# Turning q and k of head groups 7 to 23 on TensorE with the identity instead of by DMA transposes

## The chip, the cores and the metric

The kernel runs on one core of a Trainium2 chip. The metric is the device time of one execution in microseconds. The engines are named as in the profile: PE (TensorE, matrix products, with PEld for its weight loads), DVE (VectorE), ACT (ScalarE), POOL (GpSimd) and SP (SyncE, which only issues DMAs here).

## The reference

An attention with normalised q and k, followed by a two-layer network with a leaky activation:

```python
batch, n_heads, seq, head_dim = (8, 12, 448, 64)
def rmsnorm(x, g):
    rms = np.sqrt(np.mean(x * x, axis=-1, keepdims=True) + 1e-06)
    return x / rms * g
q_n, k_n = (rmsnorm(q, g_q), rmsnorm(k, g_k))
scores = scale * np.matmul(q_n, k_n.transpose(0, 1, 3, 2))     # scale = 1/8
attn = np.exp(scores - scores.max(-1)); attn = attn / (attn.sum(-1) + 1e-09)
x = np.matmul(attn, v)             # (8, 12, 448, 64) -> (3584, 768)
h = x @ w_in                       # w_in (768, 2048)
g = np.maximum(h, 0.0) + alpha * np.minimum(h, 0.0)
out = g @ w_out                    # w_out (2048, 768), out float32 (3584, 768)
```

## The kernel before

The 12 heads of each of the 8 batch entries are taken two pairs at a time as *head groups* of four heads; three groups make one batch entry, so there are 24 groups, numbered 0 to 23 (`NG`; `G` is 3). In a tile of q or k the 128 partitions are two heads by 64, and the 448 positions of the sequence are these 64 by `J` = 7.

For each group, q and k are loaded to `nat` by SP, squared by POOL (`square`), summed by DVE (`reduce`, line 185), turned into reciprocal roots by ACT (`root`), and multiplied with them by POOL into fp16 tiles `qs` (`scale`, line 205). The scores need them with the head dimension on the partitions, so q and k are *turned* into `qT` and `kT`; kT also takes the gain g_q * g_k. Then `score` makes the scores of one key block in PSUM (`sc`, line 357), `soft` takes their exp on ACT (`expT`, line 371), the denominators are sums by TensorE with a column of ones (`dn`, `dnb`), their reciprocals come from a log and an exp on ACT (`rden`), and `attv` makes the attention's product (`av`, `avb`) that DVE multiplies into `xT` (lines 464, 481).

The network is worked in between. An *up product* (`up`) is six matmuls for 128 of the 2048 inner columns and one batch entry (`hT`, line 496), then on ACT a product with alpha into gT (line 536) and on DVE a maximum with hT into gT (line 540). An *output product* is 16 matmuls (`op`, line 558) or, for most tiles, eight at a time in a scheme that saves one product in eight with sums made beforehand (`quad_a`, `quad_b`, `quad_c`: `qx`, `qz`, `qc`, line 623), copied or added out of PSUM by DVE (`osb`) and stored by SP.

The order is written out by hand, for every engine the order in the program is the order in which it works. The main loop runs over *steps* `n`. A step has two to four score blocks (`bursts`), perhaps a denominator (`dens`) and an attention product (`avs`), and then a list of network products (`gaps`), which a planner shares out by cost. `turn_at` gives the step in which a group is turned: as a rule the last step before the one with its first scores; `turns` is the same by step. `jobs` hangs small work of other engines behind network products; `late` holds back a score's exp or a group's roots until so many up products are issued.

PSUM has three pools: `pss` with two buffers of two banks for the scores, `psf` with two single banks tagged `mm`, and `psa` with one buffer of two banks tagged `acc`. Products take an `mm` bank; where the step's plan calls them `spare` they take an `acc` bank instead, and their names get an "a" (`hTa`, `opa`, `qxa`, `qza`, `qca`). Denominators (`dn`) and attention products (`av`) take `acc` too.

Groups 0 to 6 are turned by TensorE: seven transposes of 128 by 128 for q and seven for k against an identity, into PSUM, from where DVE copies q (line 337) and k with the gain (line 339). From group `TD` = 7 on (17 groups) `turn_dma` issues two transposing DMAs on SP right after the multiplications in program order (line 304), and `turn` only multiplies kT in place with the gain on DVE (line 315). In the steps of the first seven turns the planner lends no spare bank; in those of the others it does.

Of the kernel before, what the change touches and what calls it, by code (L numbers as in the profile page):

```python
# [9 lines left out]
FP32 = mybir.dt.float32  # L10
FP16 = mybir.dt.float16
AF = mybir.ActivationFunctionType
ALU = mybir.AluOpType
# [8 lines left out]
def kernel(  # L22
# [12 lines left out]
    nc = tc.nc  # L35

    B, H, S, D = q.shape
    DM = H * D
    DF = moe_w_in.shape[1]
    J = S // 64  # L40
    HH = H // 2
    G = HH // 2
# [3 lines left out]
    W = 2 * S  # L46
    NG = B * G
    FB = DF // 4
    TD = min(7, NG)
    EB = 3  # L50
    EARLY = 3 * G
    PRE = 3 * G - 1
# [145 lines left out]
    def scale(y, nm):  # L198
        if y in (1, 3, 5):
            t = lent(HB + 4 * NB4 + "qk".index(nm) * NB4 // 2, NB4 // 2).bitcast(FP16)  # L200
            t = t.rearrange("p (j h d) -> p j h d", j=J, h=2)
        else:
            t = ld.tile([128, J, 2, D], FP16, name="qs", tag="qs", bufs=2)
        eng = nc.vector if y < G or (y, nm) == (G, "q") else nc.gpsimd
        eng.tensor_mul(  # L205
            out=t.rearrange("p j h d -> p h j d"),
            in0=nat[y, nm],
            in1=rr_t[y][:, "qk".index(nm)].unsqueeze(3).broadcast_to((128, 2, J, D)),
        )
        qs[y, nm] = t  # L210
# [30 lines left out]

    def part_scale(nm, j, n, eng):
        if (0, nm) not in qs:
            qs[0, nm] = ld.tile([128, J, 2, D], FP16, name="qs", tag="qs", bufs=2)
        eng.tensor_mul(
            out=qs[0, nm][:, j].rearrange("p j h d -> p h j d"),
            in0=nat[0, nm][:, :, j],
            in1=rr_t[0][:, "qk".index(nm), :, j].unsqueeze(3).broadcast_to((128, 2, n, D)),
        )
# [9 lines left out]

    def part_copy(nm, j, eng):  # L260
        if (0, nm) not in qkT:
            qkT[0, nm] = att.tile([128, J, 2, 64], FP16, name=f"{nm}T", tag=f"{nm}T", bufs=3)
        o = qkT[0, nm].rearrange("p j g c -> p j (g c)")[:, j]
        tp = tops["ps", nm][:, j]
        if nm == "k":
            nc.vector.tensor_scalar(
                out=o, in0=tp, scalar1=gain[:, 0:1], scalar2=None, op0=ALU.mult
            )
        elif eng is nc.scalar:
            nc.scalar.copy(out=o, in_=tp)  # L270
        else:
            eng.tensor_copy(out=o, in_=tp)

    mark = cst.tile([128, 1], FP16, name="mark", tag="mark")
    mark32 = cst.tile([128, 1], FP32, name="mark32", tag="mark32")

    def follow(y, nm):

# [2 lines left out]
    def turn_one(y, nm):  # L281
        t = psf.tile([128, 512], FP32, name="tps", tag="mm")
        tp = t[:, :S].bitcast(FP16).rearrange("p (j c) -> p j c", j=J)
        for j in range(J):
            nc.tensor.transpose(
                tp[:, j, :], qs[y, nm][:, j].rearrange("p h d -> p (h d)"), ident
            )
        t = att.tile([128, J, 2, 64], FP16, name=f"{nm}T", tag=f"{nm}T", bufs=3)
        o = t.rearrange("p j g c -> p j (g c)")
        if nm == "q":  # L290
            nc.vector.tensor_copy(out=o, in_=tp)
        else:

            for c in (slice(0, 2), slice(2, J)):
                nc.vector.tensor_scalar(
                    out=o[:, c], in0=tp[:, c], scalar1=gain[:, 0:1], scalar2=None,
                    op0=ALU.mult,
                )
        qkT[y, nm] = t

    def turn_dma(y):
        for nm in "qk":
            t = att.tile([128, J, 2, 64], FP16, name=f"{nm}T", tag=f"{nm}T", bufs=3)
            nc.sync.dma_start(
                out=t.rearrange("p j g c -> p j (g c)"),
                in_=qs[y, nm].rearrange("p j h d -> p (j h d)"),
                transpose=True,
            )
            qkT[y, nm] = t

    def turn(y):

        if y >= TD:
            t = qkT[y, "k"].rearrange("p j g c -> p (j g c)")
            nc.vector.tensor_scalar(  # L315
                out=t, in0=t, scalar1=gain[:, 0:1], scalar2=None, op0=ALU.mult,
                op1=ALU.max, accum_out=mark32,
            )
            return
        if y <= G:  # L320
            ps = [psf.tile([128, 512], FP32, name="tps", tag="mm") for _ in "qk"]
        else:
            ps2 = psa.tile([128, 2, 512], FP32, name="tps2", tag="acc")
            ps = [ps2[:, 0], ps2[:, 1]]
        tps = [
            t[:, : S].bitcast(FP16).rearrange("p (j c) -> p j c", j=J) for t in ps
        ]
        for tp, nm in zip(tps, "qk"):
            for j in range(J):
                nc.tensor.transpose(  # L330
                    tp[:, j, :], qs[y, nm][:, j].rearrange("p h d -> p (h d)"), ident
                )
        for tp, nm in zip(tps, "qk"):
            t = att.tile([128, J, 2, 64], FP16, name=f"{nm}T", tag=f"{nm}T", bufs=3)
            o = t.rearrange("p j g c -> p j (g c)")
            if nm == "q":
                nc.vector.tensor_copy(out=o, in_=tp)
            else:
                nc.vector.tensor_scalar(
                    out=o, in0=tp, scalar1=gain[:, 0:1], scalar2=None, op0=ALU.mult  # L340
                )
            qkT[y, nm] = t
# [4 lines left out]
    def pre(ys):  # L347
        return len(ys) == 1 and ys[0] >= PRE and ys[0] % G == G - 1
# [428 lines left out]
    while m < NG * J or steps:  # L777
        n = len(bursts)
# [38 lines left out]
    def after(n, f, *a):  # L817
        post.setdefault(max(int(n), 0), []).append((f, a))

    turn_at = {  # L820
        y: max(n for n in range(first_in[y]) if y >= TD or n not in dens)
        for y in range(1, NG)
    }
    turn_at[2], turn_at[G] = 5, av_at[0]
    turn_at.update(
        (y, den_at[y - 2] - pre((y - 2,))) for y in range(TD, NG) if y % G == 1
    )
    turns = {n: y for y, n in turn_at.items()}
    jobs, root_at, nexts = {}, {}, {}
    for y in range(G, NG):  # L830
# [54 lines left out]
    def cost(n):  # L885
        return (
            0.31 + 0.19 * len(bursts[n])
            + (0 if n not in dens else 0.4 if pre(dens[n]) else 1.35)
            + 1.35 * len(avs.get(n, ())) + (0.9 if turns.get(n, TD) < TD else 0.0)
        )  # L890

    def wide(n):
# [152 lines left out]
    for n in range(NB):  # L1045
# [70 lines left out]
        if n in roots:  # L1116
            y = roots[n]
            work = [(root, (y,)), (scale, (y, "q")), (scale, (y, "k"))]
            if lead:

                late = [(2, score, tiles[2]), (2, soft, tiles[2])]
            if y == 2 * G:
                late += [(3, f, a) for f, a in work]
            elif lead or wait and y < TD:
                late += [(2 if lead else 1, f, a) for f, a in work]
            else:
                for f, a in work:
                    f(*a)
            if y >= TD:
                turn_dma(y)  # L1130
        if n in nexts:
            load_qk(nexts[n])
        if n in dens and not lead and not sums:
# [5 lines left out]
        done = 0  # L1139

        spare_at, clock = [], 0.0
        taken = n + 1 in dens or n + 1 in avs or turns.get(n + 1, TD) < TD
        for k, (f, a) in enumerate(gaps[n]):
            free = 2.9 if sums else 2.3 if n in dens else (0.1, 1.2, 0.0)[len(avs.get(n, ()))]
            since += 1
            if clock >= free and not turns.get(n, TD) < TD and (
                since > 2 and not (taken and k == len(gaps[n]) - 1) or free == 0.0 and k == 0
            ):
                spare_at.append(k)
                since = 0  # L1150
            clock += UP if f is up else DOWN
        ups_first = gaps[n] and gaps[n][0][0] is up
        if ups_first and n in dens and not lead:
            for f, a in jobs.pop(n, ()):
                f(*a)
        turned = n in turns and gaps[n] and (turns[n] >= TD or turns[n] <= 2 * G)
        if turned and not ups_first and turns[n] >= TD:
            jobs.setdefault(n, []).append((turn, (turns[n],)))
        elif turned:
            turn(turns[n])  # L1160
        for k, (f, a) in enumerate(gaps[n]):
            spare = k in spare_at or f is up and a in forced
            if f is down:
                down(*a, jobs.pop(n, ()), spare)
            elif f is not up:
                f(*a, jobs.pop(n, []))
            else:
                f(*a, spare)
                done += 1
                if n in jobs and not (lead and done < 5) and (  # L1170
                    n < av_at[2 * G - 1] or done % 2
                ):
                    g, c = jobs[n].pop(0)
                    g(*c)
                    if not jobs[n]:
                        del jobs[n]
                while late and done == late[0][0]:
                    _, g, c = late.pop(0)
                    g(*c)
# [50 lines left out]
```

## Time and profile before

| | |
|---|---|
| median of 3 runs | 413.47 us (413.19 to 415.29) |
| profiled execution | 414.78 us |
| its span, first to last instruction | 413.0 us |
| mean granted TensorE clock | 0.995 |
| transposing DMAs | 17 of q, 17 of k; 2.9 and 3.7 us from issue to landing (median) |

Lines of the page that help to read it further, the costliest groups of instructions (line, engine, operation, out<-in, count, then busy us and mean ns of one, then idle time before them and what ended it):

```profile
L371 ACT ACTIVATE expT<-sc 128x896 f16<-128x896 f32 x168 | 147.8, 913 | 55.4 <-PE sc L357 55.0
L496 PE MATMUL hT<-xT,w_in_sb 128*128 128x448 f16 x546 | 113.7, 353 | 0.4 <-DVE gT L540 0.2
L205 POOL TENSOR_TENSOR qs<-nat,rr 128x896 f16<-128x896 f32 x36 | 60.9, 1713 | 33.4 <-issue 24.9
```

The busy time of one engine is no time on the path by itself: what matters is which engine the others wait for. ACT waits 55 us in total for scores.

### The profile page before, as it was taken

What the parts mean: (1) busy time and instruction counts of PE and PEld (TensorE: products, weight loads), DVE (VectorE), ACT (ScalarE), POOL (GpSimd) and SP (SyncE); (2) the same over time, 40 slices, a digit from 0 to 9 for tenths busy, and PEclk for the clock granted to TensorE, in tenths of its full rate; (3) what the DMA queues carried; (4) which work ended last, traced back from release to release, by engine and by line L of the source; (5) the groups of instructions that cost most, each with busy time, mean ns of one, the idle gap of its engine ahead of it and who ended that gap; (6) DMA issues with size and microseconds to landing.
All of it is one profiled execution on the core that took longest, in us unless ns stands there. A gap on an engine that the chain in (4) does not pass through costs nothing.

```text
span 413.0 us, 11724 instructions
## 1 busy us (share of the span) xinstructions
PE 398.9 (97%) x5055; PEld 208.1 (50%) x5055; DVE 266.9 (65%) x420; ACT 257.3 (62%) x390; POOL 255.8 (62%) x184
## 2 busy tenths in 40 slices
PE   7889999899999999999999999999999999999996
PEld 3344445444456445554455445545555455645664
DVE  3876875476567388785688585958576755465322
ACT  5697787567846785557766786875657783135110
POOL 5599996589677969376373847484724407300870
PEclk9899999999999999999999999999999999999999
DMA  8999899957754894329861697279332700320143
GB/s 259 231 217 206 172 200 155 248 169 103 163 81 134 204 169 91 115 63 197 144 168 48 173 138 177 63 180 193 59 75 54 127 3 24 75 59 0 30 103 97
DMA packets 67330, 53.38 MB, mean 129 GB/s; under 512 B 34880, under 2 KB 66768, under 8 KB 67280
## 3 DMA queue, kind: packets, MB, share of 16 engines
q1 hardware_dynamic: 53344, 40.45, 40.5%
q0 software_dynamic: 13536, 11.81, 21.5%
q8 instruction: 39, 0.64, 0.7%
q10 hardware_dynamic: 400, 0.39, 0.3%
q14 instruction: 11, 0.09, 0.1%
HBM read 45.62 MB, written 11.01 MB: 137 GB/s over the span
## 4 chain that ended last, share of the span: by engine, by line
PE 49%; DVE 6%; ACT 0%; issue 0%; DVEq 0%
PE hT L496 14%; PE hTa L496 7%; PE qx L623 5%; PE sc L357 3%; PE oq L623 3%; PE qc L623 3%; PE qz L623 2%; PE av L382 2%; PE oqm L623 2%; PE avb L382 1%; PE dn L382 1%; PE oqa L623 1%; DVE ss L185 1%; DVE xT L481 1%; DVE kT L315 1%; PE qza L623 1%
## 5 line engine op out<-in xcount | busy, mean ns | idle before, releaser
L371 ACT ACTIVATE expT<-sc 128x896 f16<-128x896 f32 x168 | 147.8, 913 | 55.4 <-PE sc L357 55.0
L496 PE MATMUL hT<-xT,w_in_sb 128*128 128x448 f16 x546 | 113.7, 353 | 0.4 <-DVE gT L540 0.2
L496 PEld LDWEIGHTS <-w_in_sb 128*128 128x128 f16 x768 | 72.7, 98 | 74.8 <-issue 10.1
L540 DVE TENSOR_TENSOR gT<-hT,gT 128x448 f16<-128x448 f32 x91 | 56.6, 623 | 40.1 <-ACT gT L536 39.2
L205 POOL TENSOR_TENSOR qs<-nat,rr 128x896 f16<-128x896 f32 x36 | 60.9, 1713 | 33.4 <-issue 24.9
L536 ACT ACTIVATE gT<-hT,cols 128x448 f16<-128x448 f32 x90 | 56.9, 633 | 33.9 <-PE hT L496 33.7
L177 POOL TENSOR_TENSOR sq<-nat 128x896 f32<-128x896 f32 x32 | 53.1, 1681 | 38.0 <-DMA nat<-in_q_dram 25.3
L357 PE MATMUL sc<-qT,kT 64*32 64x448 f16 (+1 forms) x1092 | 53.3, 358 | 3.5 <-ACT expT L371 1.1
L623 PEld LDWEIGHTS <-gT 128*128 128x128 f16 x352 | 33.4, 98 | 26.0 <-issue 4.9
L496 PE MATMUL hTa<-xT,w_in_sb 128*128 128x448 f16 x210 | 45.4, 352 | 0.0
L185 DVE TENSOR_REDUCE ss<-sq 128x14 f32<-128x896 f32 (+1 forms) x37 | 38.3, 1052 | 0.6 <-POOL sq L177 0.6
L481 DVE TENSOR_TENSOR xT<-av,rden 64x448 f16<-64x448 f32 (+1 forms) x37 | 27.2, 734 | 13.5 <-PE av L382 5.5
L536 ACT ACTIVATE gT<-hTa,cols 128x448 f16<-128x448 f32 x35 | 22.2, 635 | 19.1 <-PE hTa L496 19.1
L540 DVE TENSOR_TENSOR gT<-hTa,gT 128x448 f16<-128x448 f32 x35 | 21.8, 624 | 17.7 <-ACT gT L536 17.6
L357 PEld LDWEIGHTS <-kT 64*32 64x32 f16 (+1 forms) x1092 | 15.6, 93 | 34.7 <-issue 29.3
L558 PE MATMUL op<-w_out_sb,gT 128*128 128x384 f16 x160 | 27.4, 326 | 0.0
L382 PEld LDWEIGHTS <-vt 64*32 64x32 f16 x1344 | 20.2, 92 | 14.1 <-issue 5.0
L611 POOL TENSOR_TENSOR gs<-gT 128x1024 f16<-128x1024 f16 x3 | 6.4, 2121 | 30.3 <-DVE gT L540 28.1
L558 PEld LDWEIGHTS <-gT 128*128 128x128 f16 x192 | 18.0, 98 | 13.5 <-issue 2.4
L382 PE MATMUL av<-expT,vt 64*32 64x448 f16 x896 | 24.3, 350 | 0.3 <-DVE osb L671 0.3
L619 POOL TENSOR_TENSOR gT<-gT 128x1024 f16<-128x1024 f16 x11 | 23.8, 2166 | 0.0
L623 PE MATMUL qx<-w_out_sb,gT 128*128 128x384 f16 x120 | 20.9, 326 | 0.0
(148 smaller groups left out, 494.1 us busy)
## 6 DMA issues: line engine op xcount, KB each, us to landing
out_dram<-osb SPq DMA_DIRECT2D x107, 96.0 KB, 2.8
nat<-in_k_dram SPq DMA_DIRECT2D x21, 448.0 KB, 5.4
nat<-in_q_dram SPq DMA_DIRECT2D x20, 448.0 KB, 4.9
vt<-in_v_dram POOLq DMA_DIRECT2D x8, 672.0 KB, 11.0
w_in_sb<-in_moe_w_in_dram POOLq DMA_DIRECT2D x24, 128.0 KB, 5.0
w_out_sb<-in_moe_w_out_dram POOLq DMA_DIRECT2D x4, 768.0 KB, 10.8
arena<-in_q_dram SPq DMA_DIRECT2D x3, 448.0 KB, 7.8
arena<-in_k_dram SPq DMA_DIRECT2D x3, 448.0 KB, 8.5
```

Of the source, the lines that this page charges most:

```text
L177: nc.gpsimd.tensor_mul(out=sqf[:, c], in0=src[:, c], in1=src[:, c])
L185: nc.vector.tensor_reduce(out=o[:, c], in_=sqs[y, nm][:, c], axis=AXIS_X, op=ALU.add)
L205: eng.tensor_mul(out=t.rearrange("p j h d -> p h j d"), in0=nat[y, nm], in1=rr_t[y][:, "qk".index(nm)].unsqueeze(3).broadcast_to((128, 2, ...
L357: nc.tensor.matmul(out=sc[ds(64 * g + m * c, m), par, :S].rearrange("p (j c) -> p j c", j=J), lhsT=kT[ds(64 * par, 64), j, g, ts(c, m)], r ...
L371: nc.scalar.activation(out=expT[y][:, j], in_=scs[y, j][:, :, :S], func=AF.Exp, scale=QK_SCALE, bias=EXP_BIAS,)
L382: nc.tensor.matmul(out=accs[g][ds(32 * n, 32), :S], lhsT=weights(g, y, par, c, j), rhs=expT[y][ds(64 * g, 64), j, par, :], start=(j == 0), ...
L481: nc.vector.tensor_mul(out=x, in0=av, in1=r)
L496: nc.tensor.matmul(out=hT[:, :S], lhsT=w_in_sb[:, block_of(g, i), ts(ft, 128)], rhs=xT[b][:, g, i, :], start=(i == 0 and g == 0), stop=(i ...
L536: nc.scalar.activation(out=g, in_=hT[:, :S], func=AF.Copy, scale=alpha_sb[:, ft : ft + 1])
L540: nc.vector.tensor_max(out=g, in0=hT[:, :S], in1=g)
L558: nc.tensor.matmul(out=op[:, :OH], lhsT=gT[:, ft, ts(tile % J, 128)], rhs=w_out_sb[:, ft, ts(oh, OH)], start=(ft == 0), stop=(ft == NF - 1),)
L623: nc.tensor.matmul(out=bank[:, c], lhsT=g[:, ft], rhs=v[:, ft, c], start=(first and ft == 0), stop=(ft == HF - 1), skip_group_check=True,)
```

## The change

From group 7 on the turn is made by TensorE as in the first groups. `turn_dma`, `TD` and the in-place gain are gone. The transposes go into the `acc` banks; DVE copies q and k (with the gain) out of them. `qs` has four buffers instead of two, `qT` and `kT` two instead of three. `turn_at` of all these groups is the last step before their first scores that has no denominator. In a step that has a turn, a product becomes `spare` only late in the step; in the step before, the last one does not. The turn stands ahead of the step's network products, or, in a step with an attention product, behind the first of them.

```diff
-    TD = min(7, NG)
...
-            t = ld.tile([128, J, 2, D], FP16, name="qs", tag="qs", bufs=2)
+            t = ld.tile([128, J, 2, D], FP16, name="qs", tag="qs", bufs=4)
...
-        t = att.tile([128, J, 2, 64], FP16, name=f"{nm}T", tag=f"{nm}T", bufs=3)
+        t = att.tile([128, J, 2, 64], FP16, name=f"{nm}T", tag=f"{nm}T", bufs=2)
...
-    def turn_dma(y):
-        for nm in "qk":
-            t = att.tile([128, J, 2, 64], FP16, name=f"{nm}T", tag=f"{nm}T", bufs=3)
-            nc.sync.dma_start(
-                out=t.rearrange("p j g c -> p j (g c)"),
-                in_=qs[y, nm].rearrange("p j h d -> p (j h d)"),
-                transpose=True,
-            )
-            qkT[y, nm] = t
...
     def turn(y):
-
-        if y >= TD:
-            t = qkT[y, "k"].rearrange("p j g c -> p (j g c)")
-            nc.vector.tensor_scalar(
-                out=t, in0=t, scalar1=gain[:, 0:1], scalar2=None, op0=ALU.mult,
-                op1=ALU.max, accum_out=mark32,
-            )
-            return
         if y <= G:
             ps = [psf.tile([128, 512], FP32, name="tps", tag="mm") for _ in "qk"]
         else:
...
     turn_at = {
-        y: max(n for n in range(first_in[y]) if y >= TD or n not in dens)
+        y: max(n for n in range(first_in[y]) if n not in dens)
         for y in range(1, NG)
     }
     turn_at[2], turn_at[G] = 5, av_at[0]
-    turn_at.update(
-        (y, den_at[y - 2] - pre((y - 2,))) for y in range(TD, NG) if y % G == 1
-    )
...
-            if y >= TD:
-                turn_dma(y)
...
-        taken = n + 1 in dens or n + 1 in avs or turns.get(n + 1, TD) < TD
+        taken = n + 1 in dens or n + 1 in avs or n + 1 in turns
         for k, (f, a) in enumerate(gaps[n]):
             free = 2.9 if sums else 2.3 if n in dens else (0.1, 1.2, 0.0)[len(avs.get(n, ()))]
             since += 1
-            if clock >= free and not turns.get(n, TD) < TD and (
+            if n in turns:
+                free = max(free, 2.3 if turns[n] > 2 * G + 1 else 9.0)
+            if clock >= free and (
...
-        turned = n in turns and gaps[n] and (turns[n] >= TD or turns[n] <= 2 * G)
-        if turned and not ups_first and turns[n] >= TD:
-            jobs.setdefault(n, []).append((turn, (turns[n],)))
-        elif turned:
+        behind = n in turns and n in avs
+        if n in turns and gaps[n] and not behind:
             turn(turns[n])
         for k, (f, a) in enumerate(gaps[n]):
+            if behind and k == 1:
+                turn(turns[n])
```

More of the change, by code (lines that the diff above doesn't have):

```diff
@@ L243, in part_scale @@
         if (0, nm) not in qs:
-            qs[0, nm] = ld.tile([128, J, 2, D], FP16, name="qs", tag="qs", bufs=2)
+            qs[0, nm] = ld.tile([128, J, 2, D], FP16, name="qs", tag="qs", bufs=4)
         eng.tensor_mul(
@@ L261, in part_copy @@
         if (0, nm) not in qkT:
-            qkT[0, nm] = att.tile([128, J, 2, 64], FP16, name=f"{nm}T", tag=f"{nm}T", bufs=3)
+            qkT[0, nm] = att.tile([128, J, 2, 64], FP16, name=f"{nm}T", tag=f"{nm}T", bufs=2)
         o = qkT[0, nm].rearrange("p j g c -> p j (g c)")[:, j]
@@ L274 @@
     mark = cst.tile([128, 1], FP16, name="mark", tag="mark")
-    mark32 = cst.tile([128, 1], FP32, name="mark32", tag="mark32")
     def follow(y, nm):
@@ L333, in turn @@
         for tp, nm in zip(tps, "qk"):
-            t = att.tile([128, J, 2, 64], FP16, name=f"{nm}T", tag=f"{nm}T", bufs=3)
+            t = att.tile([128, J, 2, 64], FP16, name=f"{nm}T", tag=f"{nm}T", bufs=2)
             o = t.rearrange("p j g c -> p j (g c)")
@@ L888, in cost @@
             + (0 if n not in dens else 0.4 if pre(dens[n]) else 1.35)
-            + 1.35 * len(avs.get(n, ())) + (0.9 if turns.get(n, TD) < TD else 0.0)
+            + 1.35 * len(avs.get(n, ())) + (0.9 if turns.get(n, NG) <= 2 * G else 0.0)
         )
@@ L1123 @@
                 late += [(3, f, a) for f, a in work]
-            elif lead or wait and y < TD:
+            elif lead or wait and y <= 2 * G:
                 late += [(2 if lead else 1, f, a) for f, a in work]
```

## The prediction

> **What bounds the kernel now.** I read the page first: the busy shares, then the table of stretches, then the timelines of the steps that the change touches. The page's line of TensorE:
>
> ```profile
> PE 398.9 (97%) x5055; PEld 208.1 (50%) x5055; DVE 266.9 (65%) x420; ACT 257.3 (62%) x390; POOL 255.8 (62%) x184
> ```
>
> TensorE's matmul row is nearly full and no other engine is over 65%. A matmul's end is modelled, so 97% alone proves little; the stretches from 80 us on, in which all 17 turns by DMA are used, say more:
>
> ```profile
> core 0: us, PE busy (x) PEld busy (x) DVE busy (x) ACT busy (x) POOL busy (x), PEclk, DMA share, GB/s
> 80.00:140.00 60.00, 59.83 (x782) 31.01 (x782) 37.56 (x58) 41.27 (x64) 50.17 (x32) 1.00 0.60 135
> 140.00:200.00 60.00, 59.54 (x756) 30.47 (x753) 45.40 (x70) 39.70 (x61) 39.69 (x24) 1.00 0.72 139
> 200.00:260.00 60.00, 59.16 (x932) 30.70 (x917) 44.62 (x68) 43.42 (x65) 36.86 (x22) 1.00 0.70 147
> 260.00:320.00 60.00, 59.30 (x855) 31.38 (x853) 42.61 (x71) 40.53 (x62) 32.61 (x20) 1.00 0.54 101
> ```
>
> Each stretch of 60 us has under 0.9 us of TensorE idle, at a granted clock of 1.00; up to 380 us the idle time is 300 - 297.55 = 2.45 us. The groups start at a fixed pace (six up matmuls every 1.13 to 1.15 us) whether the DMA share is 0.96 (180 to 200 us) or 0.13 (360 to 380 us). So TensorE is the bound, and a DMA transpose costs it nothing now: what the change adds to its stream comes straight on top.
>
> **The added transposes.** Groups 7 to 23, 17 of them, need 7 transposes of q and 7 of k each: 17 x 14 = 238 matmuls with their weight loads; the built program has these 238 more and no DMA transpose. The kernel already turns its first groups so, and that gives the price:
>
> ```profile
> 58.40 0.57 PE L357 MATMUL sc<-qT,kT 64*64 64x448 f16 x8
> 58.91 0.95 PE L330 MATMUL tps<-ident,arena 128*128 128x128 f16 x14
> 59.70 2.43 PE L496 MATMUL hT<-xT,w_in_sb 128*128 128x448 f16 x12
> ```
>
> From the start of 14 transposes to that of the next matmul: 59.70 - 58.91 = 0.79 us, 56 ns each (a turn before an output product, 62.84 to 63.63 us, gives 0.79 too). The row's own mean of 219 ns is the latency, not the pace. 17 x 0.79 = 13.4 us, all on the path. The Trainium skill ("TensorE: Matmul & The Clock Gate", "Back-to-back issue gap") says that a stream of weight load and 128-column matmul pairs runs at about 81 ns each, and that the 56 ns of a lone matmul under-counts. By that the term would be 238 x 0.081 = 19.3 us; the rows above, which are such a stream, show the 56 ns.
>
> **VectorE.** It loses the in-place gain on kT and gets two copies out of PSUM:
>
> ```profile
> L315 DVE TENSOR_SCALAR_CACHE_REDUCE kT<-kT,gain 128x896 f16<-128x896 f16 x17 | 19.3, 1135 | 0.0
> L339 DVE TENSOR_SCALAR kT<-tps,gain 128x896 f16<-128x896 f16 x5 | 3.4, 676 | 0.0
> L337 DVE COPY qT<-tps 128x896 f16<-128x896 f16 x5 | 3.1, 621 | 0.7 <-PE tps L330 0.6
> ```
>
> Out go 1135 ns and 82 ns for reading the accumulator, 1.22 us a turn; in come 676 + 621 = 1.30 us: 17 x 0.08 = 1.4 us more in an engine at 65%. I cost the sum at nothing; what counts is what waits behind the copies (below).
>
> **PSUM banks, first wait.** Each turn now takes the two banks tagged acc, which in the same steps lent a third bank to the up products (hTa). In the built program 26 up products use it instead of 35. What a bank's round costs is seen here:
>
> ```profile
> 100.82 1.31 PE L496 MATMUL hT<-xT,w_in_sb 128*128 128x448 f16 x6
> ...
> 101.97 1.30 PE L496 MATMUL hTa<-xT,w_in_sb 128*128 128x448 f16 x6
> 102.17 0.63 ACT L536 ACTIVATE gT<-hT,cols 128x448 f16<-128x448 f32 x1 [0.30 <-PE hT L496]
> ...
> 102.83 0.62 DVE L540 TENSOR_TENSOR gT<-hT,gT 128x448 f16<-128x448 f32 x1
> ...
> 103.38 1.07 DVE L185 TENSOR_REDUCE ss<-sq 128x14 f32<-128x896 f32 x1
> ```
>
> TensorE leaves the bank at 101.97; ScalarE and then VectorE have emptied it at 102.83 + 0.62 = 103.45, 1.48 us later, and some 0.04 us more pass before TensorE starts (issue rows of the chain). The next up product takes only 1.13 us. With three banks in turn this is hidden; on two banks the third of a row waits 1.52 - 1.13 = 0.39 us. The built order has five turn steps with four up products in a row on two banks (groups 8, 11, 12, 15, 17) and five with three (9, 14, 18, 21, 23). In a step of four the fourth also waits: an exp (0.91 us) stands on ScalarE between the first two evictions, and in three of them a reduce (1.07 us) on VectorE. Laid out row by row from the rows above, the fourth waits 0.3 us without a reduce and 0.5 us with one: 0.7 to 0.9 a step, say 0.8. Sum: 5 x 0.8 + 5 x 0.39 = 6.0 us. Bounds: 2 us if half the groups find their bank free early, 11 us if each of the 15 waits is 0.75, as where a reduce comes first.
>
> **PSUM banks, second wait.** In the steps behind an attention product (groups 10, 13, 16, 19, 22) the acc banks are asked for again soon. At group 13:
>
> ```profile
> 171.11 0.55 DVE L669 TENSOR_TENSOR osb<-qz,osb 128x384 f32<-128x384 f32 x1
> 171.34 1.47 PE L623 MATMUL qc<-arena,gT 128*128 128x384 f16 x8
> 171.58 0.55 DVE L671 TENSOR_TENSOR osb<-qz,osb 128x384 f32<-128x384 f32 x1
> 172.04 1.07 DVE L185 TENSOR_REDUCE ss<-sq 128x14 f32<-128x896 f32 x1
> 172.65 1.46 PE L623 MATMUL qca<-w_out_sb,s 128*128 128x384 f16 x8
> ```
>
> The transposes come in at 171.34, end at 172.13, qc runs to 173.43. VectorE is free of the reduce at 173.04, and the two copies, 1.22 us back to back (24.93 to 26.16 us at an early turn), end near 174.3. Only then may qca, which has the acc banks, start: 0.85 us of wait. At group 19 an up product (1.13 us) in place of qc makes it 1.0; at 16 and 22 the waiting product comes one later in VectorE's favour and some 0.3 is left; at 10 the transposes wait for the copy out of opa (it ends at 124.5, they arrive at 124.17): 0.35. Sum 2.8 us; bounds 0 and 7 (two reduces of 1.07 ahead of the copies in three places). Behind each wait the whole TensorE stream stands, scores and products alike; nothing overtakes.
>
> **What is taken away.** On SP's queue 34 transposes of 1.22 us each, so loads and stores no longer stand behind them; 4.3 us in which GpSimd waited for them before it wrote qs; VectorE's place for kT. All lie off the path: TensorE has 2.45 us of idle in 300. I take 0.5 us back; bounds 0 and 2.4. The scaled q and k are ready in time: for group 9, the closest, GpSimd ends at 104.67 and TensorE, even without its added work, gets to the turn at 105.97. Twice the qs buffers (bufs 4) cover the later reading, and two qT and kT are enough, since scores of a group end before the turn after next. If GpSimd were late by one 1.69 us multiplication, each such group would cost that much; I cost it at nothing.
>
> **Sum.** 13.4 + 6.0 + 2.8 - 0.5 = 21.7 us. The profiled execution took 414.78 us with a span of 413.0; it would become 436.5. The median of the runs, 1.3 us lower at 413.47, becomes 435.2 us.
>
> **Rivals.** *The waits hide* (chance 0.14): a wait in a step makes the next evictions less late, and scores between the products give the banks time. For it: before, pairs of up products with 0.50 us of scores between them never wait. Against: in the steps named, nothing stands between. Time 413.47 + 13.4 - 0.5 = 426 to 428 us. *The acc banks become the second bound* (0.14): the copies stand behind reduces and evictions, and each late copy delays the next. For it: VectorE does up to 2 us of reduces in one go (121.97, 2.07 us). Against: VectorE is idle for 35%. Upper ends: 13.4 + 11 + 7 = 31.4, so 445 us. *TensorE takes the transposes in its bubbles* (0.04, the only way to faster): its weight loads show 50%, and without the transposing DMAs the 2.45 us of idle could close too. Time 413.47 - 2.4 = 411 us if the transposes are free; it decides if a transpose costs under 2.45 / 238 = 10 ns, against 56 in the rows. The Trainium skill ("Perfetto Trace Analysis", "Identifying the Most-Contended Engine") holds that matmul occupancy is a poor measure of TensorE's room and weight-load occupancy a better one, by which VectorE's 65% would be the limit here; the fixed pace of the groups speaks against it. That the change does not do what it says is ruled out by the built program's instructions.
>
> **How the numbers follow.** The forecast with its waits has 0.68. Half of 0.04, with the transposes half free, is still within 0.5% (about what a measurement of this kernel can tell from no change), half faster: faster 0.02, same 0.02, slower 0.96. The range runs from the hidden waits, 426, to near the upper ends of the waits, 444.
>
> **What would show it.** In the profile after: 238 more transposes with a pace of 0.79 us per 14; no transposing DMA; TensorE's idle from 80 us to the end of scores up from about 2.5 to some 10 us, put down to VectorE's gT (L540) and to qT and kT copies; hT waits at the third and fourth product of a turn step. Wrong would be: 14 transposes in other than 0.75 to 0.9 us, idle under 4 us or over 20, waits on GpSimd's qs, or up groups at another pace than 1.13 us.

## The result, and the profile after

The changed kernel takes 436.06 us (median of 4 runs, 435.21 to 436.83), the kernel before 413.58 us in the same comparison (4 runs): 1.0535 times as long, 95% interval 1.0496 to 1.0573. The forecast was 435.2 us.

The profiled execution took 435.21 us, its span is 433.4 us, 20.4 us more than before. The page's line of TensorE after:

```profile
PE 414.4 (96%) x5293; PEld 220.3 (51%) x5293; DVE 265.9 (61%) x420; ACT 257.5 (59%) x390; POOL 255.9 (59%) x184
```

5293 - 5055 = 238 more matmuls. VectorE, ScalarE and GpSimd have the same busy microseconds as before to within 1 us; only TensorE has more. The same four stretches as in the prediction (busy us of each engine, granted clock, DMA share, GB/s):

```profile
80.00:140.00 60.00, 58.26 (x757) 31.12 (x755) 35.01 (x54) 36.42 (x56) 44.50 (x29) 1.00 0.30 74
140.00:200.00 60.00, 57.25 (x745) 30.47 (x743) 38.69 (x61) 36.78 (x58) 43.19 (x26) 1.00 0.44 114
200.00:260.00 60.00, 57.80 (x770) 30.47 (x769) 42.53 (x67) 40.17 (x62) 27.29 (x17) 1.00 0.39 92
260.00:320.00 60.00, 58.37 (x842) 31.50 (x848) 38.23 (x62) 37.78 (x56) 37.42 (x22) 1.00 0.33 81
```

TensorE's idle time in them is 240 - 231.68 = 8.3 us, where it was 2.2 us; the DMA share is about half of what it was. The engine is as much the bound as before, with more to do and with new waits. Who made it wait (total us, times, longest):

```profile
PE hT L476 <- DVE gT L520: 4.6, 14, 1.0
...
PE hTa L476 <- DVE kT L319: 0.9, 1, 0.9
PE qca L603 <- DVE kT L319: 0.8, 1, 0.8
...
PE qza L603 <- DVE kT L319: 0.3, 1, 0.3
PE tps L310 <- DVE osb L549: 0.3, 1, 0.3
```

The first line is the wait of the up products on two banks, 14 times, where 15 were forecast; the others are waits for the `acc` banks. None is for a DMA or for GpSimd's `qs` in the changed groups. The turn step of group 8 shows both parts of the added time (start, us, engine, line):

```profile
99.95 0.57 PE L337 MATMUL sc<-qT,kT 64*64 64x448 f16 x8
100.46 0.95 PE L310 MATMUL tps<-ident,qs 128*128 128x128 f16 x14
101.25 2.43 PE L476 MATMUL hT<-xT,w_in_sb 128*128 128x448 f16 x12
103.93 1.29 PE L476 MATMUL hT<-xT,w_in_sb 128*128 128x448 f16 x6 [0.25 <-DVE gT L520]
105.45 1.30 PE L476 MATMUL hT<-xT,w_in_sb 128*128 128x448 f16 x6 [0.23 <-DVE gT L520]
```

The transposes take 101.25 - 100.46 = 0.79 us. Two up products then run to 101.25 + 2 x 1.135 = 103.52, the third starts at 103.93 (0.41 us late), and the fourth 105.45 - 103.93 - 1.135 = 0.39 us late. (The bracket says less, 0.25 and 0.23, because the modelled end of a matmul lies about 0.16 us after TensorE could have started the next.)

To compare kernels without what differs from run to run in the loads at the start, I take the *stage* from the first matmul of the first product named opa to the last score matmul; all 17 changed turns lie in it. Before it runs from 76.67 to 344.77 us, 268.1 us; after from 74.85 to 365.06, 290.2 us: 22.1 us more, of the 22.5 us between the medians.

### The profile page after: what moved, and what is told of

Same layout as the page of the kernel before. It is cut to its first block, busy times and chain, and to the rows that moved or that the text cites. A ratio compares the mean times of both kernels' runs of the same rounds, so it can differ in the third digit from the quotient of the medians.

```text
span 433.4 us, 12141 instructions
## 1 busy us (share of the span) xinstructions
PE 414.4 (96%) x5293; PEld 220.3 (51%) x5293; DVE 265.9 (61%) x420; ACT 257.5 (59%) x390; POOL 255.9 (59%) x184
## 5 line engine op out<-in xcount | busy, mean ns | idle before, releaser
L476 PE MATMUL hT<-xT,w_in_sb 128*128 128x448 f16 x600 | 124.8, 352 | 4.7 <-DVE gT L520 4.6
L520 DVE TENSOR_TENSOR gT<-hT,gT 128x448 f16<-128x448 f32 x100 | 62.2, 623 | 50.8 <-ACT gT L516 50.5
L516 ACT ACTIVATE gT<-hT,cols 128x448 f16<-128x448 f32 x99 | 62.7, 634 | 50.9 <-PE hT L476 50.8
L476 PE MATMUL hTa<-xT,w_in_sb 128*128 128x448 f16 x156 | 33.8, 353 | 0.9 <-DVE kT L319 0.9
L516 ACT ACTIVATE gT<-hTa,cols 128x448 f16<-128x448 f32 x26 | 16.5, 636 | 21.4 <-PE hTa L476 21.4
L520 DVE TENSOR_TENSOR gT<-hTa,gT 128x448 f16<-128x448 f32 x26 | 16.2, 625 | 16.0 <-ACT gT L516 16.0
```

Source lines behind the costliest of these rows:

```text
L476: nc.tensor.matmul(out=hT[:, :S], lhsT=w_in_sb[:, block_of(g, i), ts(ft, 128)], rhs=xT[b][:, g, i, :], start=(i == 0 and g == 0), stop=(i ...
L516: nc.scalar.activation(out=g, in_=hT[:, :S], func=AF.Copy, scale=alpha_sb[:, ft : ft + 1])
L520: nc.vector.tensor_max(out=g, in0=hT[:, :S], in1=g)
```

## The experiments

Each run is set against the kernel before, timed beside it (412.8 to 413.1 us median); *after* is the changed kernel.

**Transposes alone.** To the kernel before, 14 transposes of weight columns in each turn step, into the acc banks, read by nobody:

```diff
         if y >= TD:
+            extra(y)
             t = qkT[y, "k"].rearrange("p j g c -> p (j g c)")
...
+    def extra(y):
+        ps2 = psa.tile([128, 2, 512], FP32, name="tps2", tag="acc")
+        for n in range(2):
+            tp = ps2[:, n, :S].bitcast(FP16).rearrange("p (j c) -> p j c", j=J)
+            for j in range(J):
+                nc.tensor.transpose(tp[:, j, :], w_in_sb[:, n, ts(j, 128)], ident)
```

> The kernel before, with its DMA turns, and in each of the 17 turn steps 14 more transposes of weight columns into the acc banks, which nobody reads (they replace no work; the result is as before). My theory: they cost 17 x 0.79 = 13.4 us and nothing else, since no copy holds the banks and the up products keep their third bank: 413.6 + 13.4 = 427 us, give or take 1. The rival that TensorE has room in its bubbles: 413 to 416 us. The rival that the waits, not the transposes, make most of the 22 us: well under 420 us.

Measured 431.13 us (1.0435, interval 1.0383 to 1.0487), more than expected. In the profiled execution (430.21 us) the stage is 283.2 us, 15.1 more than before. (The medians differ by 18.2 us, with runs from 428.0 to 432.7; one profile doesn't show where the other 3 us come from.) The price of the transposes was right, 0.78 to 0.79 us to the next matmul wherever nothing else waits, but my placing of them made waits that I had not counted: they ask for the acc banks where an up or an attention product still holds them.

```profile
199.00 0.57 PE L365 MATMUL sc<-qT,kT 64*32 64x448 f16 x16
200.45 0.94 PE L316 MATMUL tps<-ident,w_in_sb 128*128 128x128 f16 x14 [0.88 <-DVE gT L548]
201.23 1.11 PE L504 MATMUL hT<-xT,w_in_sb 128*128 128x448 f16 x5
```

Here the transposes wait 0.88 us and then take 0.78; three more such waits are 0.5 us each in the profile's reading, for the reciprocals of the attention product, and five turns lose some 0.2 us. TensorE has no room for the transposes, and "413 to 416" falls. That "nothing else" is paid for does not hold: even without copies two banks have to be had.

**Two banks, by DMA.** The kernel before, with DMA turns, under the spare rule of the changed kernel:

```diff
+    turn_steps = {
+        max(n for n in range(first_in[y]) if n not in dens): y for y in range(1, NG)
+    }
+    turn_steps.update((turn_at[y], y) for y in (2, G))
...
-        taken = n + 1 in dens or n + 1 in avs or turns.get(n + 1, TD) < TD
+        taken = n + 1 in dens or n + 1 in avs or n + 1 in turn_steps
...
+            if n in turn_steps:
+                free = max(free, 2.3 if turn_steps[n] > 2 * G + 1 else 9.0)
-            if clock >= free and not turns.get(n, TD) < TD and (
+            if clock >= free and (
```

> The kernel before with its DMA turns and without any transpose on TensorE in groups 7 to 23, but with the spare rule of the changed kernel: the same up products go without the third bank (26 use it, as after). My theory: the waits of the up products on two banks appear without any transpose, some 14 of 0.4 to 0.9 us, so 413.6 + 5 to 7 = 419 to 421 us. The rival that these waits come from the copies of qT and kT in VectorE's queue and not from the number of banks: within 1.5 us of before.

Measured 417.61 us (1.0118, 1.0095 to 1.0141), the stage 273.1 us, 5.0 more. TensorE's waits:

```profile
PE hT L496 <- DVE gT L540: 4.2, 14, 1.0
```

The same 14 waits in the same places, with no transpose and no copy in these steps: the number of banks makes them, not the copies. From start to start they have the size that they have in the changed kernel to within 0.06 us, but for the one at group 18, 0.53 us here and 0.87 there. The longest, 1.13 us at group 12, is here too, behind a subtraction of weights on VectorE:

```profile
152.01 2.02 DVE L591 TENSOR_TENSOR w_out_sb<-w_out_sb 128x768 f16<-128x768 f16 x1
...
154.62 1.67 PE L496 MATMUL hT<-xT,w_in_sb 128*128 128x448 f16 x8 [0.97 <-DVE gT L540]
```

The time is 1.4 us under the expected range, since some of the waits of the kernel before went at the same time (0.9 us of avb for osb the largest). From group 8 on the same up products as in the changed kernel go without the third bank; over the whole run 27 use it, not 26.

**The third bank back.** One number of the changed kernel:

```diff
-                free = max(free, 2.3 if turns[n] > 2 * G + 1 else 9.0)
+                free = max(free, 2.2 if turns[n] > 2 * G + 1 else 9.0)
```

> The changed kernel with one number changed: in turn steps a product may be spare from 2.2 us of the planner's clock on instead of 2.3, which gives the third of four up products the acc banks again in the five turn steps with four in a row (groups 8, 11, 12, 15, 17) and shifts one in groups 14 and 23. My theory: the waits of hT on VectorE's gT in these steps, 5.0 to 5.5 us by the profile of the changed kernel, go, since the copies out of acc end 1.5 us after the transposes and the third product comes 2.3 us after them: 436.1 - 5.2 = 431 us. The rival that the copies hold acc too long: the wait moves from hT to hTa and the time stays within 1 us of 436.

Measured 432.7 us (1.0483, 1.0451 to 1.0515); the stage is 286.5 us, 3.7 us less than after. The waits went from 14 to 4, but a part came back in front of the bank that was to help:

```profile
PE hT L476 <- DVE gT L520: 1.8, 4, 1.1
PE hTa L476 <- DVE kT L319: 1.7, 2, 0.9
```

In group 12 the third product now stands in front of the acc banks for 0.88 us instead of in front of the mm bank. VectorE's queue shows why:

```profile
157.94 2.43 PE L476 MATMUL hT<-xT,w_in_sb 128*128 128x448 f16 x12
...
158.34 1.73 DVE L571 TENSOR_TENSOR w_out_sb<-w_out_sb 128x768 f16<-128x768 f16 x1
...
160.00 0.61 DVE L317 COPY qT<-tps 128x896 f16<-128x896 f16 x1
160.53 0.67 DVE L319 TENSOR_SCALAR kT<-tps,gain 128x896 f16<-128x896 f16 x1
...
161.25 1.31 PE L476 MATMUL hTa<-xT,w_in_sb 128*128 128x448 f16 x6 [0.88 <-DVE kT L319]
```

The copies could start at 158.1 and start at 160.0, behind a subtraction of weights. The wait of group 18's third product grew by 0.4 us. So both held in part: the banks are worth most of what I said, and the rest is that group 12's wait stayed, now for a late copy, and that group 18's grew.

**The copy of q on ScalarE.** The changed kernel, for every third group:

```diff
-            if nm == "q":
+            if nm == "q" and y > 2 * G and y % G == 1:
+                nc.scalar.copy(out=o, in_=tp)
+            elif nm == "q":
                 nc.vector.tensor_copy(out=o, in_=tp)
```

> The changed kernel, with the copy of q out of PSUM on ScalarE instead of VectorE for groups 7, 10, 13, 16, 19 and 22 (every third). My theory: the acc banks are free about 0.55 us earlier there, so the waits for kT's copy in front of qca (0.95 us, group 13), hTa (1.03, group 19), qza (0.49 and 0.26, groups 22 and 16) and the scores of group 7 (0.78) shrink to 0.5 us or nothing: 2.2 us less than the changed kernel, 434 us; group 10, which waits for opa's copy, stays. The rival that these waits are VectorE's earlier queue alone: no difference over 0.7 us.

It did not gain: 437.09 us (1.0588, 1.055 to 1.0625), the stage 291.6 us, 1.4 us over after. At group 13:

```profile
180.00 1.73 ACT L353 ACTIVATE expT<-sc 128x896 f16<-128x896 f32 x2 [2.10 <-PE sc L339]
...
181.61 0.91 ACT L317 COPY qT<-tps 128x896 f16<-128x896 f16 x1
...
182.56 0.68 DVE L321 TENSOR_SCALAR kT<-tps,gain 128x896 f16<-128x896 f16 x1 [0.73 <-ACT qT L317]
...
183.30 1.46 PE L605 MATMUL qca<-w_out_sb,s 128*128 128x384 f16 x8 [0.99 <-DVE kT L321]
```

The copy takes 0.91 us on ScalarE instead of 0.62, begins behind two exps, and VectorE's copy of k out of the same tile waits until it is done. Two readers of the tile went one after the other, so the wait grew from 0.79 to 0.99 us. At groups 16 and 22 it grew too (by 0.9 and 0.7 us), at 19 it shrank by 0.3, and at 7 and 10 nothing changed. What the expectation was to tell apart, the copies or the queue ahead of them, is not decided by this run.

**Both mends together.** The bank back, and q's copy on ScalarE in all 17 groups:

> The changed kernel with both mends: the third of four up products takes the acc banks again, and the copy of q out of PSUM is on ScalarE in all of groups 7 to 23. My theory: the kernel with the bank mended (432.7 us) loses another 2.9 us of waits behind kT's copy (2.2 as above, 0.6 of the 1.05 in front of hTa in group 12): 430 us, and what is left over before is the 13.4 us of transposes and 3 to 4 us of waits; faster than before it cannot be. The rival that ScalarE's copies make the exps and gT products late: 432 us or more.

432.87 us (1.0482, 1.0446 to 1.0517), the same as the third bank alone; the stage is 287.3 us. The best of these is still 4.8% above the kernel before.

**Each transpose twice.** In the changed kernel every one of the 238 is issued twice into the same place:

```diff
-            for j in range(J):
+            for j in [j for j in range(J) for _ in range(2 if y > 2 * G else 1)]:
```

> The changed kernel with each of the 238 transposes of groups 7 to 23 issued twice in a row into the same place (same result). My theory: another 17 x 0.79 = 13.4 us, all on the path, and the waits neither grow nor shrink by more than 1 us: 449.5 us. The rival that the transposes lie partly in time that TensorE waits anyway: under 445 us. The rival by a rate of 81 ns each: 436.1 + 19.3 = 455 us.

446.17 us (1.0815, 1.0776 to 1.0854): 10.1 us above after by the medians, 9.8 us by the stage (300.0 us). This refutes the second half of my expectation. 28 transposes take 1.56 to 1.57 us, as they should, 13.3 us more in all, but the waits shrank by the missing 3.5 us. At group 13:

```profile
183.61 1.74 PE L310 MATMUL tps<-ident,qs 128*128 128x128 f16 x28
...
184.31 1.08 DVE L184 TENSOR_REDUCE ss<-sq 128x14 f32<-128x896 f32 x1
185.18 1.46 PE L603 MATMUL qc<-arena,gT 128*128 128x384 f16 x8
185.38 0.62 DVE L317 COPY qT<-tps 128x896 f16<-128x896 f16 x1
185.93 0.68 DVE L319 TENSOR_SCALAR kT<-tps,gain 128x896 f16<-128x896 f16 x1
...
186.75 1.46 PE L603 MATMUL qca<-w_out_sb,s 128*128 128x384 f16 x8
```

While TensorE turns twice, VectorE gets through its reduce; the copies start 0.20 us after the transposes, and qca waits 186.75 - 185.18 - 1.30 = 0.27 us in all instead of the 0.95 us of the changed kernel. The 14 waits of hT on two banks remain (3.4 us, longest 0.2); the two long ones, at groups 12 and 18, fell to 0.41 us each from start to start. So the second kind of wait is a backlog of VectorE at the moment of the turn, which the reduces ahead of the copies make; more work on TensorE eats it up.

**The DMA turns, more of them.** Two runs on whether the transposing DMAs cost the kernel before anything. First all 34 twice into the same tile:

```diff
-            nc.sync.dma_start(
+            for _ in range(2):
+                nc.sync.dma_start(
```

> The kernel before with each of the 34 transposing DMAs issued twice, one after the other, into the same tile (same result). My theory: the DMA turns lie off the path, and twice as many stay off it: within 1 us of 413.6. The rival that the transposing DMAs cost the kernel before something, which the change gives back: slower by at least 2 us.

476.25 us (1.1551, 1.1468 to 1.1635), far off. The second transpose waits on SP's queue until the first has landed, and everything behind it waits too:

```profile
107.76 1.22 SPq L305 DMA_TRANSPOSE kT<-qs  x1
...
111.20 6.38 SPq L305 DMA_TRANSPOSE qT<-qs  x2
115.16 1.15 DVE L316 TENSOR_SCALAR_CACHE_REDUCE kT<-kT,gain 128x896 f16<-128x896 f16 x1 [7.18 <-DMA kT<-qs]
...
116.23 0.62 DVE L541 TENSOR_TENSOR gT<-hT,gT 128x448 f16<-128x448 f32 x1
...
116.91 1.65 PE L497 MATMUL hT<-xT,w_in_sb 128*128 128x448 f16 x4 [6.24 <-DVE gT L541]
```

kT's gain stands on VectorE in front of a maximum, so a transpose that lands late stops the up products for 6.24 us. This says that the DMA turn lies off the path only as long as it lands in time, not what its traffic costs. The second run, 17 more without that wait:

```diff
             qkT[y, nm] = t
+            if nm == "q":
+                more = att.tile([128, J, 2, 64], FP16, name="more", tag="more", bufs=1)
+                nc.sync.dma_start(
+                    out=more.rearrange("p j g c -> p j (g c)"),
+                    in_=qs[y, nm].rearrange("p j h d -> p (j h d)"),
+                    transpose=True,
+                )
...
-        return ffn.tile([128, OH], FP32, name="osb", tag="osb", bufs=6)
+        return ffn.tile([128, OH], FP32, name="osb", tag="osb", bufs=5)
```

> The kernel before with 17 more transposing DMAs: each qs of q is turned a second time into a tile that nobody reads, so that no transpose waits for another one's landing on its tile as in the kernel with each issued twice (to make room, osb has five buffers instead of six). My theory: the transposing DMAs' traffic lies off the path: within 2 us of before. The rival that the DMA engines' time or SP's queue is the narrow place behind the 63 us of the run with all 34 twice: 10 us or more above before.

417.44 us (1.0112, 1.0046 to 1.0178), between the two theories: 4.3 us. The control with five osb buffers alone:

> The kernel before with five osb buffers instead of six and nothing else: the control for the run with 17 more transposing DMAs, which was 4.3 us slower than before. If the fewer buffers made that, this run is 416 to 418 us; if the added DMAs did, it is within 1 us of before. By the profile of that run, in which no wait of TensorE in the stage of the DMA turns is put down to a store, I expect the latter: 413 us.

413.49 us (1.0014, 0.999 to 1.0039), as expected, so the added DMAs made nearly all of it. In the profile of the run with them TensorE's two longest waits in the stage are 1.7 us in an output product, put down to nothing that the profile shows ("issue"), and 1.1 us for VectorE's copy of a denominator. So half as many transposing DMAs again cost about 1%; by what path they cost it stays open, since the longest of these waits is put down to nothing. What the 34 cost at their own number was not measured by taking them away alone. In the stage of the kernel before no wait of TensorE is put down to them, and most of what TensorE got back in the changed kernel it also got back in a run that keeps them (see below).

## Why the prediction was right

**The bound and the transposes.** TensorE is the bound: right. 17 x 0.79 = 13.4 us: right in all 17 turns (0.78 or 0.79 us each). The 81 ns of the Trainium skill ("TensorE: Matmul & The Clock Gate", "Back-to-back issue gap") would have been 6 us too much here. The pace of the up products stayed at 1.13 us with half the DMA share, and no traffic relief shows in it. The run with the transposes doubled bears out the price and limits the sum: the same again, 13.3 us, came to only 10.1 (9.8 in the stage), since they ran partly into waits. The terms of my sum were not independent; the transposes' own price was counted beside waits that would have been longer without them.

**First wait, two banks.** Forecast 15 waits and 6.0 us. Found are 14 of these 15 places (at group 12 the fourth product does not wait, since the third has waited so long) and one more in the step before group 14's turn: 7.1 us of lost pace from start to start (4.6 us in the profile's own reading, which lists 14 and leaves out one of 0.2 us). The wait at group 21, 0.41 us, was not new: the kernel before has it in the same place. So 6.7 us were added. The 0.41 and 0.39 us of one step are the 0.39 and 0.3 to 0.5 that were worked out. The excess is in groups 12 and 18 (1.18 and 0.87 us in one wait each). In group 12 a subtraction of weights on VectorE, ahead of the copies, took 1.72 us where it had taken 0.55; the run with two banks by DMA has 1.13 us of this wait without any copy. Of group 18's it has 0.53 us, so some 0.3 us there can be the copies'.

**Second wait, the acc banks.** Group 13: 0.85 forecast, 0.95 found; group 19: 1.0 and 1.03; groups 16 and 22: 0.3 each, 0.26 and 0.49; group 10: 0.35, 0.39. Sum 2.8 forecast, 3.1 found. Not foreseen: the scores of group 7 wait 0.7 us for kT, and an output product of group 20 waits 0.47 us behind the copies, 0.13 us of which it had waited before. Together they add 1.0 us of the same kind. (The turn of group 15 also waits 0.2 us, for an up product in acc, but in the kernel before an up product waited as long in its place.)

**What is given back.** I took 0.5 us. With TensorE's matmuls of before and after laid side by side in their order, the waits of before that are gone in the stage come to 2.0 us (0.9 us of avb for osb, the others under 0.3 each): inside the bounds, but four times the term, which was mis-sized. 1.6 of the 2.0 us are also gone in the run with the transposes alone, which keeps all 34 DMA turns, so most of it is not what the transposing DMAs had cost. 13.4 + 6.7 + 3.1 + 1.0 = 24.2, less 2.0, is 22.2 against the stage's 22.1. The waits came out 2.0 us over the forecast and what is given back 1.5 us over; that these nearly cancel, so that the sum came this close, is luck.

**Rivals.** That the waits hide (426 to 428) is refuted by the run with DMA turns and two banks; that the acc banks become a second bound is true in small: with VectorE's backlog they cost some 4 us, and 445 would have taken 9 us more. That TensorE takes the transposes in its bubbles is refuted by the transposes alone: the kernel slowed by their full price. So the rule of the Trainium skill ("Perfetto Trace Analysis", "Identifying the Most-Contended Engine"), that weight-load occupancy (50% before, 51% after) shows TensorE's room, does not hold here.

## What to carry to other kernels

Where one engine's instructions follow each other without a gap, price an added instruction by the start-to-start pace of the same group elsewhere in the trace, not by its duration (56 against 219 ns), and add it in full; take off only the waits that it will fill (the second 13.3 us of transposes cost 9.8 us). Then ask which buffers it takes: here the PSUM banks that the turns took from the up products cost half as much as the turns' own matmuls, 6.7 against 13.4 us, and one number in the planner gave 3.7 us back. A transfer that lands in time stays off the path, but it is only as cheap as its margin: find the instruction that waits for it and what stands behind that in its queue.

## What the runs showed of the hardware that I had not expected

The same fp16 subtraction of 128x768 elements on VectorE took 0.549 us before and 1.724 us after. After, GpSimd was in a multiplication at the time; before, GpSimd was idle:

```profile
156.92 1.68 POOL L176 TENSOR_TENSOR sq<-nat 128x896 f32<-128x896 f32 x1 [0.99 <-DVE ss L184]
158.55 2.00 POOL L204 TENSOR_TENSOR qs<-nat,rr 128x896 f16<-128x896 f32 x1
```

It ran from 157.29 to 159.01 us; the GpSimd multiplication that began during it took 2.00 us instead of 1.69. The Trainium skill ("GPSIMD Engine Reference", "1. Specifications") says that GpSimd's SBUF interfaces are shared with VectorE and contend with VectorE instructions that have two SBUF inputs, as this one has; the trace agrees.

The runs also show how the time is lost. In seven of them, after among them, a GpSimd multiplication was under way when the subtraction began, 1.00, 1.31 or 1.60 us before its end. The subtraction took 1.42, 1.72 and 2.02 us, and each time it ended 0.41 us after that multiplication; in the four runs with GpSimd idle there it took 0.55 us. So by these times it stood still until GpSimd was through, and did not merely run slower.

In the run with every transposing DMA twice, in which TensorE stood still for up to 6 us at a time, the granted clock was 0.91 to 0.97 in the stretches from 80 to 380 us, where it is 1.00 in all the others. Waits of 1 us, as the changed kernel has, left it at 1.00.
